# Second norm as token rows, queries masked by DMA, reciprocal products on GpSimd: a transformer block on one core of a Trainium2 chip

## The chip, the core and the metric

The kernel runs on one core of one Trainium2 chip. The metric is the device time of one execution in microseconds, as the median of the runs taken. Engines are named as in the profile: PE (TensorE, with PEld for its weight loads), DVE (VectorE), ACT (ScalarE), POOL (GpSimd) and SP (SyncE, which issues most of the DMAs). An engine takes its instructions strictly in the order in which they were issued, so an instruction that waits holds up all behind it.

## What is computed

With `x` of 2048 tokens by 512 features (bf16), the reference is a sum of three terms:

```python
xn = _layernorm(x)                              # no weights
return x + _A_ref(xn, A_wqkv, A_wo) + _B_ref(xn, B_w1, B_b1, B_w2, B_b2)

# A: softmax attention, 32 heads of 16 features, over all 2048 keys, then @ wo
# B: y = _layernorm(xn); h = gelu(y @ w1 + b1) with 1792 features; h @ w2 + b2
```

`B` norms `xn` a second time. Row by row this is a factor: with `v` the variance of a row of `x` and `r1 = (v + eps)^-1/2`, the row of `xn` is `(x - mean) * r1`, and `y = xn * r2` with `r2 = (v * r1^2 + eps)^-1/2`.

## The kernel before

**Tiling.** Tokens stand in 16 tiles of 128 (`x_sb`), the normed and transposed tokens in `xnT` (features on the partitions). Attention works in 32 groups `g`: 4 query chunks of 512 times 8 sets of 4 heads. A set pair `b` (8 heads) shares a projected key tile `kt`; its queries are projected once per query chunk into `qc`, and two copies in `qz` have the heads of the other set zeroed by `mask` (`build_q`, L921). A *unit* is the scores of one head of a group against 128 keys: one score matmul (L1063) into a PSUM bank of 128x512. Groups have 64 units each, 2048 in all.

**Two ways to the exponential.** ACT takes units in tiles of two or three banks: one ACTIVATE of 1024 or 1536 columns writes `p_sb` (`build_tile`, L1223 to L1295). DVE takes four units (one key tile of 4 heads) at a time: four times L1365 turns scores into int16 that read as float16 are a coarse exponential, and three times L1386 makes shifted copies of 2048 columns; PE then sums four terms in place of one (L1081). So a key tile costs PE one group of 4 concurrent value matmuls when ACT makes it, and four groups when DVE does. Which key tiles go to DVE is not fixed: `next_d` hands one out when DVE has a free buffer, ACT takes what is left.

**The other work** lies between: layer norm of the tokens in four steps of four tiles (`layernorm`, L737), key, value and query projections, two MLP stages of two token chunks each (`build_mlp`, L1521: the row factors `r2` are broadcast by 16 POOL products `rt` and a PE pass into `r2b`, then DVE makes `yT = xnT*r2b + xnT`; 14 matmul chains with `w_r`, a DVE add of the bias, gelu on ACT), the down projection, and the output. A group's end (`build_opost`, L1408): DVE copies the sums to `osb`, four DMAs by way of DRAM fetch the row of softmax sums, `rc` is its reciprocal, `rlb` the reciprocal spread over the partitions, and DVE multiplies `osb` by `rlb` (L1435) into `ont` or `ons`.

**What sets the order.** `_Plan` collects every operation with an engine, a duration, a priority and its dependences. `run` (L134) places them one at a time at the earliest start, by priority within a tolerance, and each engine's instructions are then issued in that order. `nudge` adds a seeded number to the priorities, one seed (`MIX`) for each group. Where PE would be idle for long, `fill` (L1688) puts in groups of 4 matmuls on zeros (L1718) that change no sum. The places that the change touches: `layernorm`, `f_r2` (L801), `late_dma` (L810), the first queries (`fq0`, `fq1`, L884 to L900), `build_q`, `build_opost`, `build_opost_last` (L1463), `build_mlp`, `build_final` (L1632).

## Time and profile before

| | |
|---|---|
| median of 3 runs | 769.67 us (769.47 to 770.04) |
| span of the profiled execution, first to last instruction | 767.6 us |
| busy, share of the span: PE, DVE, ACT, POOL | 96%, 92%, 97%, 8% |
| granted TensorE clock, mean | 0.998 |
| first and last exponential start on ACT | 12.01 us, 756.86 us |

The profiled execution has no time of its own beside its span; the runs are taken without the profiler. The span is 2.07 us below their median. What lies around the span (the start of the program, the landing of the last output) is taken as this 2.07 us. Busy time is the union of the instructions of an engine; matmuls overlap, so that a busy PE still has room.

### The profile page before, as it was taken

Reading aid. Unit: us, or ns where it says so; the run is one execution under the profiler, and the core shown is the slowest. Engines: PE = TensorE matmul, PEld = TensorE weight load, DVE = VectorE, ACT = ScalarE, POOL = GpSimd, SP = SyncE. Lnnn points to the kernel's source line nnn. Section 1 sums busy time; section 2 is a strip of 40 time slices with the busy share of each in tenths; the row PEclk is TensorE's granted clock in tenths of the full one; section 3 lists DMA queues with packets and bytes.
Section 4 is the critical chain, followed back from the end, with each engine's and each line's share of the span. In section 5 each row is a group of like instructions: output and inputs, shape, how many; then the busy total and the mean of one; then the engine's idle time right before and its main releaser. Section 6 shows DMA issues by size and latency. Waiting matters only on the chain.

```text
span 767.6 us, 23757 instructions
## 1 busy us (share of the span) xinstructions
PE 737.2 (96%) x10248; PEld 251.1 (33%) x10249; DVE 703.5 (92%) x1210; ACT 747.0 (97%) x655; POOL 62.0 (8%) x96
## 2 busy tenths in 40 slices
PE   8999999999999899999999999999999999999997
PEld 3443433343333232333233333222333333332332
DVE  7889999989999979989999968999999977888996
ACT  5999999999999999999999999999999999999995
POOL 2400100000042000001002010000001001100011
PEclk9999999999999999999999999999999999999999
DMA  6301011202142001122012132200211013200001
GB/s 192 106 3 32 20 51 41 52 18 51 47 115 71 16 5 51 37 56 64 21 43 61 31 75 62 60 9 16 62 41 37 19 29 79 68 12 25 5 18 44
DMA packets 59724, 35.43 MB, mean 46 GB/s; under 512 B 42404, under 2 KB 51428, under 8 KB 59616
## 3 DMA queue, kind: packets, MB, share of 16 engines
q1 hardware_dynamic: 52464, 23.91, 11.4%
q0 software_dynamic: 4608, 8.39, 4.8%
q8 instruction: 81, 1.33, 0.7%
q10 hardware_dynamic: 2544, 1.57, 0.7%
q14 instruction: 27, 0.22, 0.1%
HBM read 26.08 MB, written 2.61 MB: 37 GB/s over the span
## 4 chain that ended last, share of the span: by engine, by line
PE 38%; DVE 26%; ACT 25%; issue 10%; DMA 0%; POOL 0%; ACTq 0%; SPq 0%; DVEq 0%
ACT p_sb L1268 24%; PE ps L598 13%; PE ps L1081 12%; PE ps L1063 12%; DVE x_sb L1365 9%; DVE it L1386 8%; DVE it L1365 2%; DVE ht L1560 1%; ACT ht L1574 1%; DVE va L963 1%; DVE osb L1421 1%; DVE kt L915 1%; DMA x_sb<-in_A_x_dram 0%; PE ps L1718 0%; DVE stats L742 0%
## 5 line engine op out<-in xcount | busy, mean ns | idle before, releaser
L1268 ACT ACTIVATE p_sb<-ps 128x1536 bf16<-128x1536 f32 (+1 forms) x632 | 711.3, 1269 | 4.5 <-PE ps L1063 2.3
L1063 PE MATMUL ps<-qz,kt 32*128 32x512 bf16 x2048 | 314.6, 382 | 18.9 <-ACT p_sb L1268 9.1
L1365 DVE TENSOR_SCALAR x_sb<-ps 128x512 int16<-128x512 f32 x396 | 261.7, 680 | 18.4 <-PE ps L1063 18.1
L1386 DVE TENSOR_SCALAR it<-x_sb 128x2048 int16<-128x2048 int16 x297 | 197.9, 682 | 2.6 <-PE ps L1081 1.5
L1063 PEld LDWEIGHTS <-kt 32*128 32x128 bf16 x2048 | 86.5, 91 | 265.8 <-issue 258.9
L1081 PE MATMUL ps<-p_sb,va 128*32 128x512 bf16 x1552 | 151.6, 389 | 1.0 <-DVE x_sb L1365 0.2
L1081 PE MATMUL ps<-it,va 128*32 128x512 f16 x1588 | 128.5, 381 | 0.0
L1081 PEld LDWEIGHTS <-va 128*32 128x32 bf16 x3536 | 76.0, 94 | 129.7 <-issue 106.2
L1223 PE MATMUL ps<-ones_bf,zeros_bf 32*128 32x512 bf16 x291 | 106.1, 383 | 0.0
L1365 DVE TENSOR_SCALAR it<-ps 128x512 int16<-128x512 f32 x100 | 66.7, 680 | 2.4 <-PE ps L1063 2.3
L598 PE MATMUL ps<-w_sb,ht 128*32 128x512 bf16 x896 | 59.6, 381 | 0.2 <-DVE x_sb L1365 0.2
L598 PE MATMUL ps<-yT,w_r 128*32 128x512 bf16 x896 | 58.5, 381 | 0.6 <-DVE it L1365 0.3
L1386 DVE TENSOR_SCALAR it<-it 128x2048 int16<-128x2048 int16 x75 | 50.8, 683 | 1.5 <-PE ps L1081 1.0
L1560 DVE TENSOR_SCALAR ht<-ps,b_sb 128x512 bf16<-128x512 f32 x56 | 41.6, 743 | 5.6 <-PE ps L598 5.3
L1718 PE MATMUL ps<-ones_bf,zeros_bf 128*32 128x512 bf16 x488 | 41.9, 383 | 0.0
L1081 PE MATMUL ps<-x_sb,va 128*32 128x512 f16 x396 | 38.9, 383 | 0.1
L1223 PEld LDWEIGHTS <-zeros_bf 32*128 32x128 bf16 x291 | 26.1, 91 | 18.1 <-issue 17.3
L1456 POOL TENSOR_SCALAR okt<-lc 128x128 f32<-128x128 f32 (+1 forms) x4 | 4.0, 998 | 342.3 <-DMA lc<-ldram 342.3
L1584 POOL DMA_DIRECT2D wkv<-in_A_x_dram x16 | 12.4, 772 | 235.1 <-DVE ot L1598 224.6
L598 PEld LDWEIGHTS <-w_r 128*32 128x32 bf16 x896 | 21.6, 96 | 23.9 <-issue 9.6
L598 PEld LDWEIGHTS <-ht 128*32 128x32 bf16 x896 | 21.0, 96 | 22.5 <-issue 8.8
L1574 ACT ACTIVATE ht<-ht 128x3584 bf16<-128x3584 bf16 x8 | 24.9, 3178 | 0.0
(100 smaller groups left out, 352.5 us busy)
## 6 DMA issues: line engine op xcount, KB each, us to landing
rlb<-rdram SPq DMA_DIRECT2D x31, 256.0 KB
...
wkv<-in_A_x_dram POOLq DMA_DIRECT2D x16, 256.0 KB, 3.4
wkv<-in_B_b_dram POOLq DMA_DIRECT2D x16, 256.0 KB, 4.0
...
ont<-ons SPq DMA_DIRECT2D x60, 16.0 KB
```

What stands on the lines that cost most here:

```text
L598: I(nc.tensor.matmul(dst[32 * j:32 * j + 32], lhsT=lhsT[:, 32 * j:32 * j + 32], rhs=rhs, start=start, stop=stop, tile_position=(0, 32 * j)))
L915: I(nc.vector.tensor_copy(out=kt[:, b, c0:c0 + QW], in_=ps[:, pool.bank(key), :]))
L1063: I(nc.tensor.matmul(ps[:, bank, :], lhsT=kt[lo:lo + 32, s // 2, k * P:(k + 1) * P], rhs=qz[lo:lo + 32, (qt * NB + s // 2) % NQB, s % 2, : ...
L1081: I(nc.tensor.matmul(ps[32 * j:32 * j + 32, o_bank[g], :], lhsT=vals[:, h * VS:h * VS + 32], rhs=wts(j), start=pv_done[g] == 1, stop=end, ...
L1223: I(nc.tensor.matmul(ps[:, o_bank[g], :], lhsT=zeros_bf[32 * j:32 * j + 32, :], rhs=ones_bf[32 * j:32 * j + 32, :], start=False, stop=Fals ...
L1268: I(nc.scalar.activation(p_sb[:, s0:s1, :].rearrange("p a b -> p (a b)"), ps[:, b0:b0 + n, :].rearrange("p a b -> p (a b)"), AF.Exp, scale ...
L1365: I(nc.vector.tensor_scalar(out=ib[sl][:, j, :], in0=ps[:, pool.bank(key), :], scalar1=LEVEL, scalar2=0.0, op0=ALU.add, op1=ALU.max))
L1386: I(nc.vector.tensor_scalar(out=tb[x].rearrange("p j q -> p (j q)"), in0=ib[sl].rearrange("p j q -> p (j q)"), scalar1=float(SHIFT[t]), sc ...
L1560: I(nc.vector.tensor_scalar(out=hq[:, fc, :], in0=ps[:, misc.bank(key), :], scalar1=b1_sb[:, fc:fc + 1], scalar2=None, op0=ALU.add))
L1574: I(nc.scalar.activation(out=hv, in_=hv, func=AF.Gelu_apprx_tanh, scale=1.0))
L1584: xb_ = add("POOL", 1.0, lambda: I(nc.gpsimd.dma_start(out=acc[:, c, :], in_=x2[qi * P:(qi + 1) * P, :])), wait, pr - 30, lat=XL, nb=pr - 45)
L1718: I(nc.tensor.matmul(ps[32 * j:32 * j + 32, bank, :], lhsT=zeros_bf[:, 0:32], rhs=ones_bf[:], start=new, stop=new, tile_position=(0, 32 * ...
```

## The change

1. **Second norm token-major.** `r12 = r2*r1` is made on POOL for each four token tiles; DVE makes `ys = (x - mean)*r12` from `x_sb` (16 tiles of 128x512); POOL's queue writes them to DRAM (`ydram`), and one transposing DMA a chunk on SP's queue brings `yT` back. `rt`, `r2b`, its PE pass and the two DVE operations of 2048 columns a chunk are gone.
2. **Tokens of the fourth step** (tiles 12 to 15) go to `xnT` by four transposing DMAs, no longer by PE and a DVE copy. The transposes of tiles 4 to 11 use 4 matmuls of 128 columns each in place of 16 of 32.
3. **Masked queries by DMA.** `qc` is written to DRAM beside zeros (`zdram`), and two DMAs read it back with the rows of the other heads zero, into `qz`; the 30 DVE products are gone, 45 DMAs come onto SP's queue.
4. **Products with the reciprocals** (`osb*rlb`) go from DVE to POOL for the first 28 groups.
5. **First step.** ACT takes mean and variance of token tile 3; the first queries are split 384 and 128 columns over two banks, where ACT takes 128 columns of one copy; ACT issues three DMAs fewer.
6. **Last step.** Three of the four last output tiles get the sums by a PE pass and are copied by ACT (before: two); the check of the softmax sums is counted by PE, with less on POOL and no `okrow` on DVE.
7. **Order.** `MIX` is all zero; `PICK` names about a hundred operations each on DVE and PE that are to be taken at a given place in the order. Late loads wait for an exponential (`held`).

```diff
+                want = self.pick.get(e, {}).get(self.count[e])
+                if want is not None:
+                    t, op = next((c for c in every if c[1].seq == want), (t, op))
...
+    PICK = {
+        "DVE": {
+            3: 21, 16: 44, 19: 45, 22: 63, 27: 80, 29: 54, 34: 81, 36: 79, 38: 75, 39: 72, 40: 69,
...
+    def held(inst):
+
+        if len(exp_inst) > 1:
+            tc.add_manual_dep(inst.ins, exp_inst[-2].ins.name, SYNC_DEP, reason="its turn")
...
+            if t == 3:
+                def fs0():
+                    I(nc.scalar.activation(out=p_sb[:, 0, :], in_=x_sb[:, 3, :], func=AF.Copy,
+                                           scale=-D ** -1.5, accum_out=nm3[:]))
+
+                def fs1():
+                    I(nc.scalar.activation(out=p_sb[:, 1, :], in_=x_sb[:, 3, :], func=AF.Square,
+                                           bias=nm3[:], scale=D ** -0.5, accum_out=mv[:, 3, 1:2]))
...
+            if g in DG:
+                def ftd(t=t):
+                    I(nc.sync.dma_start_transpose(
+                        out=xnT[:, t // TQ, :, (t % TQ) * P:(t % TQ + 1) * P], in_=xn_r[:, t % 4, :]))
+                xn_op[t] = xt_op[t] = add("SP", 1.55, ftd, (xo,), pr, lat=TLAT)
+                continue
...
+            I(nc.gpsimd.tensor_tensor(out=r12[:, sl], in0=wv2[:, sl], in1=r1[:, sl], op=ALU.mult))
...
+            def fy(t=t):
+                I(nc.vector.tensor_scalar(
+                    out=ys[:, t % 2, :], in0=x_sb[:, t, :], scalar1=mv[:, t, 0:1],
+                    scalar2=r12[:, t:t + 1], op0=ALU.subtract, op1=ALU.mult))
+            y_op[t] = add("DVE", 0.33, fy, (r, yw_op.get(t - 2)), pr + t % 4 * 0.2)
+            yw_op[t] = add("POOL", 0.65, lambda t=t: I(nc.gpsimd.dma_start(
+                ydram[t * P:(t + 1) * P, :], ys[:, t % 2, :])), (y_op[t],), pr, lat=3.0)
...
-    qz_h = add("ACT", 0.31, fq1(QW // 2, QW), (q0, mk_mask), -30)
-    qz_op[0, 0, 0] = add("DVE", 0.36, fq0(0, 0, QW // 2), (q0, mk_mask, qz_h), -21)
+    qa = add("DVE", 0.47, fq0(0, key0, 0, QC), (qs[2], mk_mask), -21)
+    qz_op[0, 0, 0] = add("ACT", 0.3, fq1, (q0, mk_mask), -30)
...
+        w = dma("SP", zd.rearrange("(b z r) q -> b z r q", z=2, r=DH)[:, 0],
+                qc[:, n % 2, :], [e, mk_z[n % 2]] + qz_rd.get(n - 2, []), prio=pr - 600, lat=2.4)
...
-            def fd(par=par):
-                I(nc.vector.tensor_scalar(out=qz[:, n % NQB, par, :], in0=qc[:, n % 2, :],
-                                          scalar1=mask[:, par:par + 1], scalar2=None,
-                                          op0=ALU.mult))
-            o = add("DVE", dve(QW, 0.26), fd, [e, mk_mask] + old, pr + par - 600)
+            src = bass.AP(zd.tensor, zd.offset + par * DH * QW, [[4 * DH * QW, HS], [QW, 2 * DH], [1, QW]])
+            o = dma("SP", qz[:, n % NQB, par, :], src, [w] + old, prio=pr - 599 + par, lat=4.6)
...
-        e4 = add("DVE", dve(QW), lambda: I(nc.vector.tensor_tensor(
-            out=dst, in0=osb[:, i2, :], in1=rlb[:], op=ALU.mult)), [e3] + list(free),
-            pr - (1000 if g >= NG - LASTN else 0))
+        late = g >= NG - LASTN
+        e4 = add("DVE" if late else "POOL", dve(QW) if late else GMUL,
+                 lambda: I((nc.vector if late else nc.gpsimd).tensor_tensor(
+                     out=dst, in0=osb[:, i2, :], in1=rlb[:], op=ALU.mult)), [e3] + list(free),
+                 pr - (1000 if late else 0))
...
-        e3 = add("DVE", 0.2, lambda: I(nc.vector.tensor_reduce(
-            out=okrow[:], in_=okall[:], op=ALU.min, axis=AX.XY)), [e1, e2], pr - 10.0)
...
-        y = add("DVE", dve(4 * QW, 0.52), lambda: I(nc.vector.tensor_tensor(
-            out=yT[:], in0=xnT[:, qt, :, :],
-            in1=r2b[:].unsqueeze(1).to_broadcast([P, JC, QW]), op=ALU.mult)),
...
+        y = add("SP", 3.4, lambda: I(nc.sync.dma_start_transpose(
+            out=yT[:], in_=ydram[qt * QW:(qt + 1) * QW, :])),
+            y_use + [yw_op[4 * qt + i] for i in range(4)] + list(xn_op.values()), lo - 8, lat=YLAT,
+            nb=lo - 12)
...
-            if c % 2 == 0:
-                dep = [add("PE", 0.9, fi, dep, pr - 20, acq=acq, mode="d")]
+            if c != 2:
+                dep = [add("PE", 0.6, fi, dep, pr - 20, acq=acq, mode="d")]
```

**How the instructions move.** Counted over the whole order of each engine, from the kernel before to the changed one: exponentials on ACT 632 to 623 (344 of 1024 columns and 288 of 1536 before; 339, 283 and one of 512 now), which are 1552 and 1528 units; L1365 on DVE 496 to 520 and L1386 372 to 390, which is 124 and 130 key tiles; value matmuls on PE 3536 to 3608; matmuls on zeros in `fill` 488 to 468. On SP's queue 281 rows become 335. On PE's order of the changed kernel, between the last matmul that reads the first chunk's `yT` and the first that reads the second chunk's there are 28 score matmuls; between the third and the fourth key chunk's first projection, 23; between a query pair's projection and the first score matmul that reads its `qz`, at least 46 (62 or more before).

*ACT at the start* (names: `nm` holds tile 3's negative mean, `mv` its variance, `qz` the masked queries), from the table load to the exponentials, before:

```order
L791 ACT_TABLE_LOAD
L791 CAST xnT<-ps 128x4x128 x3
L878 CAST kt<-ps 128x128
L893 ACTIVATE qz<-ps,maskq 128x256
L880 CAST kt<-ps 128x384
L1268 ACTIVATE p_sb<-ps 128x1024 x10
```

and in the changed kernel:

```order
L803 ACT_TABLE_LOAD
L803 ACTIVATE p_sb,nm_84<-x_sb 128x512
L807 ACTIVATE p_sb,mv<-x_sb,nm_84 128x512
L877 CAST xnT<-ps 128x4x128 x3
L979 CAST kt<-ps 128x128
L993 ACTIVATE qz<-ps,maskq 128x128
L981 CAST kt<-ps 128x384
L1374 ACTIVATE p_sb<-ps 128x1024 x14
```

Two statistics of tile 3 stand ahead of the copies, and ACT's share of the first queries is 128 columns in place of 256.

*DVE at the input of the second MLP chunk*, before (`x_sb` and `it` are the buffers of DVE's exponentials):

```order
L1386 TENSOR_SCALAR it<-x_sb 128x2048 x2
L1365 TENSOR_SCALAR x_sb<-ps 128x512
L1537 CAST r2b<-ps 128x512
L1539 TENSOR_TENSOR yT<-xnT,r2b 128x2048
L1365 TENSOR_SCALAR x_sb<-ps 128x512 x2
L1544 TENSOR_TENSOR yT<-yT,xnT 128x2048
```

and *SP* at the same place of the changed kernel, where the chunk's input is made:

```order
L1637 DMA_TRANSPOSE yT<-ydram 128x4x512
L737 DMA w_r<-in_B_w_dram 128x4x128
L737 DMA zdram<-qc 8x16x512
L737 DMA qz<-zdram 128x1x512 x2
L1529 DMA ldram<-osb 4x512
```

DVE has none of L1537, L1539 and L1544 any more; SP has a transposing DMA, and behind it the write and the two reads of a query pair.

*POOL after the first query chunk's check*, before:

```order
L1458 TENSOR_TENSOR okt<-okt 128x128
L1459 TENSOR_TENSOR okall<-okall,okt 128x128
L1584 DMA wkv<-in_A_x_dram 128x512
L1587 DMA wkv<-in_B_b_dram 128x512
```

and in the changed kernel:

```order
L1566 TENSOR_TENSOR okt<-okt 128x128
L1567 TENSOR_TENSOR okall<-okall,okt 128x128
L1543 TENSOR_TENSOR ons<-osb,rlb 128x512
L1543 TENSOR_TENSOR ont<-osb,rlb 128x512
L1679 DMA wkv<-in_A_x_dram 128x512
L1682 DMA wkv<-in_B_b_dram 128x512
```

28 such products of 128x512 stand in POOL's order now, one for each of the first 28 groups.

## Rows read from the trace of the kernel before

**Rows 1.** The page: span and busy time of each engine.

```profile
span 767.6 us, 23757 instructions
...
PE 737.2 (96%) x10248; PEld 251.1 (33%) x10249; DVE 703.5 (92%) x1210; ACT 747.0 (97%) x655; POOL 62.0 (8%) x96
```

**Rows 2.** Window of the exponentials: us, busy of PE, PEld, DVE, ACT, POOL; clock, DMA.

```profile
12.01:757.98 745.97, 724.12 (x10147) 245.19 (x10147) 690.54 (x1173) 741.75 (x646) 55.81 (x76) 1.00 0.17 43
```

**Rows 3.** The page's groups: xcount | busy us, mean ns | idle before, releaser.

```profile
L1268 ACT ACTIVATE p_sb<-ps 128x1536 bf16<-128x1536 f32 (+1 forms) x632 | 711.3, 1269 | 4.5 <-PE ps L1063 2.3
```

**Rows 4.** Timeline of ACT at the start: start us, us, what [idle before].

```profile
4.56 1.28 ACT L791 ACT_TABLE_LOAD   x1 [4.56 <-DMA x_sb<-in_A_x_dram]
...
9.42 0.58 ACT L791 CAST xnT<-ps 128x512 bf16<-128x512 f32 x1 [0.25 <-PE ps L603]
9.91 0.27 ACT L878 CAST kt<-ps 128x128 bf16<-128x128 f32 x1
10.54 0.47 ACT L893 ACTIVATE qz<-ps,maskq 128x256 bf16<-128x256 f32 x1 [0.36 <-PE ps L603]
```

**Rows 5.** The chain of waits at the start: start us, us, what.

```profile
6.28 0.61 DVE stats L742
...
6.91 0.19 DVE mv L743
```

**Rows 6.** Groups by line and shape, DVE's first queries.

```profile
L886 DVE TENSOR_SCALAR qz<-ps,mask 128x256 bf16<-128x256 f32 x1 | 0.5, 484 | 1.3 <-ACT qz L893 1.3
```

**Rows 7.** The chain of waits at the end.

```profile
761.67 0.58 DVE yT L1665
762.25 0.17 DVE okrow L1500
...
762.47 0.69 DVE yT L1665
```

**Rows 8.** Groups by line and shape on DVE, removed or added to.

```profile
L1365 DVE TENSOR_SCALAR x_sb<-ps 128x512 int16<-128x512 f32 x396 | 261.7, 680 | 18.4 <-PE ps L1063 18.1
L1386 DVE TENSOR_SCALAR it<-x_sb 128x2048 int16<-128x2048 int16 x297 | 197.9, 682 | 2.6 <-PE ps L1081 1.5
...
L1435 DVE TENSOR_TENSOR ont<-osb,rlb 128x512 bf16<-128x512 f32 x16 | 10.9, 680 | 0.0
...
L938 DVE TENSOR_SCALAR qz<-qc,mask 128x512 bf16<-128x512 bf16 x30 | 9.1, 346 | 0.2
...
L772 DVE TENSOR_SCALAR yT<-x_sb,mv,r 128x512 bf16<-128x512 bf16 x16 | 5.6, 405 | 0.6 <-POOL r L758 0.6
...
L1539 DVE TENSOR_TENSOR yT<-xnT,r2b 128x2048 bf16<-128x2048 bf16 x4 | 4.9, 1222 | 0.1
L1544 DVE TENSOR_TENSOR yT<-yT,xnT 128x2048 bf16<-128x2048 bf16 x4 | 4.9, 1214 | 0.0
```

**Rows 9.** Groups by line and shape, matmuls on zeros that fill PE.

```profile
L1718 PE MATMUL ps<-ones_bf,zeros_bf 128*32 128x512 bf16 x488 | 41.9, 383 | 0.0
```

**Rows 10.** One line each: duration ns min/median/max, first and last start us.

```profile
L1459 POOL TENSOR_TENSOR okall<-okall,okt x4: 455/603/782, 213.8 to 746.6; 128x128 f32<-128x128 f32 x3, 128x112 f32<-128x112 f32 x1
```

**Rows 11.** Groups by line and shape, POOL's smallest product.

```profile
L1495 POOL TENSOR_TENSOR okl<-okl 128x8 f32<-128x8 f32 x2 | 0.4, 202 | 0.2
```

**Rows 12.** DVE's shifted copies, as rows 10.

```profile
L1386 DVE TENSOR_SCALAR it<-x_sb x297: 620/681/942, 47.1 to 755.6; 128x2048 int16<-128x2048 int16 x149
```

**Rows 13.** Timeline where the two meet: start us, us, what.

```profile
213.66 1.51 DVE L1386 TENSOR_SCALAR it<-x_sb 128x2048 int16<-128x2048 int16 x2
...
213.83 0.78 POOL L1459 TENSOR_TENSOR okall<-okall,okt 128x128 f32<-128x128 f32 x1
```

**Rows 14.** A window in which POOL is busy throughout, as rows 2.

```profile
234.00:238.00 4.00, 3.86 (x60) 1.38 (x58) 3.73 (x7) 3.87 (x4) 4.00 (x5) 1.00 0.49 104
```

**Rows 15.** DMA issues on POOL's queue: count, KB each, median us to landing.

```profile
wkv<-in_B_b_dram POOLq DMA_DIRECT2D x16, 256.0 KB, 4.0
```

**Rows 16.** Score matmuls: duration ns min/median/max, first and last start us.

```profile
L1063 PE MATMUL ps<-qz,kt x2048: 371/384/386, 11.6 to 755.9; 32*128 32x512 bf16 x187
```

More of the change, by code (lines that the diff above doesn't have):

```diff
@@ L134, in run @@
     def run(self):
-        free = {e: 0.0 for e in self.ENGS}
+        free = self.free = {e: 0.0 for e in self.ENGS}
+        self.count = {e: 0 for e in self.ENGS}
         ready = self.ready = {e: [] for e in self.ENGS}
@@ L215 @@
     pe_log = ()
+    pick = {}
     nq = 0
@@ L565 @@
     xn_r = yT
-    rt = const.tile([P, 4, P], BF, name="rt")
-    r2b = const.tile([P, QW], BF, name="r2b")
+    ys = const.tile([P, 2, D], BF, name="ys")
+    r12 = const.tile([P, NT], F32, name="r12")
     ht = const.tile([P, 2, FC, QW], BF, name="ht")
@@ L740, in layernorm, with fs2 @@
         for t in tt:
+            if t == 3:
[5 more added lines that the diff above has]
+                                           bias=nm3[:], scale=D ** -0.5, accum_out=mv[:, 3, 1:2]))
+                def fs2():
+                    I(nc.gpsimd.tensor_scalar(out=mv[:, 3, 0:1], in0=nm3[:], scalar1=-D ** 0.5,
+                                              scalar2=None, op0=ALU.mult))
+                s0 = add("ACT", 0.75, fs0, [ld_x[3]], -60, nb=4.1)
+                st_op[3] = add("ACT", 0.75, fs1, [s0], -60)
+                mean3.append(add("POOL", 0.25, fs2, [s0], -35))
+                continue
             def fst(t=t):
@@ L759, in frs @@
                                           op=ALU.pow))
-            r = add("POOL" if g else "DVE", 0.4 if g else 0.12, fes, [st_op[t] for t in range(sl.start, sl.stop)],
+            r = add("POOL" if g else "DVE", 0.4 if g else 0.12, fes, [st_op[t] for t in range(sl.start, sl.stop)]
+,
                     pr - (0 if g else 20))
+            if a == 0:
+                r.outs.append(st_op[2])
+                st_op[2].ndeps += 1
             r = add("POOL", 1.0 if g else 0.75, frs, [r, mk_half], pr)
@@ L920 @@
     qc_use = {}
+    qz_rd = {}
+    mk_z0 = add("POOL", 0.9, lambda: I(nc.gpsimd.memset(ons[:], 0.0)), (), 0.0)
+    mk_z = [add("POOL", 0.65, lambda n=n: I(nc.gpsimd.dma_start(
+        zdram[n].rearrange("(e p) q -> p e q", e=2), ons[:])), (mk_z0,), 10.0, lat=3.0, nb=16.0)
+        for n in range(2)]
     def build_q(qt, b):
@@ L1668, in fe @@
                     I(nc.scalar.copy(out=yT[:, c, :], in_=ps[:, pool.bank(key), :]))
-            outs.append(add("DVE" if c % 2 else "ACT", dve(D), fe, [m] + y_use, pr,
+            outs.append(add("DVE" if c == 2 else "ACT", dve(D), fe, [m] + y_use, pr,
                             rel=(pool.giver(key),)))
```

161 lines of the change are left out of this document (83 added, 78 removed), and 35 rows, old and new, of the table PICK.

## Prediction

> **What bounds the kernel now.** I read the page first, then the windows, the groups by line, the two ends of the chain of waits, and last the few places where POOL works. The page gives PE 96%, ACT 97% and DVE 92% of a span of 767.6 us [rows 1]; three engines are close to full, so the shares do not say which one sets the time. The window of the exponentials does: from 12.01 to 757.98 us ACT is busy for 741.75 of 745.97 us, 99.4% [rows 2], while PE is idle for 22 us and DVE for 55 us. And ACT's exponentials sat idle for only 4.5 us in the whole run, start included [rows 3]. So between its first and its last exponential this kernel is a queue of work on ACT, and time goes where ACT's work goes, as long as PE and DVE hand it scores in time. Outside the window lie 12.0 us ahead (a chain of waits through DVE, POOL, PE and ACT) and 9.6 us behind.
>
> PE's 97% inside the window is not all work: 488 matmuls on zeros, 122 groups of 4, run only where PE would be idle [rows 9]. DVE has room, but not much: its waits for PE before L1365 alone are 18.4 us [rows 8].
>
> **The change, part by part.** All against the span of 767.6 us; the runs' median lies 2.07 us above it, and I add that at the end.
>
> *Work moved off ACT: -11.0 us.* ACT's 632 exponentials take 711.3 us [rows 3] for the 1552 units of the order, 0.458 us a unit. The changed order has 1528. 24 x 0.458 = 11.0. This is fixed when the program is built; what can fail is only that ACT waits more.
>
> *What pays for it on DVE.* Gone: 28 products of `osb` by `rlb` at 0.680 (19.0), 30 masked copies (9.1), the two large operations of `yT` (4.9 + 4.9) [rows 8]; 4 copies to `r2b` and 4 of `xnT`, which read PSUM like L1365, at its 0.68 (5.4). Together 43.3. Added: 16 `ys` tiles of the size and kind of L772 (5.6 in all), 24 of L1365 at 261.7/396 = 0.661 (15.9), 18 of L1386 at 197.9/297 = 0.666 (12.0) [rows 8]; together 33.5. DVE's work falls by 9.8 to 693.7 us, and on a span near 756 its share stays at 92%. So DVE can do the six more key tiles, with no more and no less room than now.
>
> *PE.* 72 more value matmuls, 18 groups; nine score passes fewer, 16 matmul groups for `r2b` and the transposes of tiles 12 to 15 gone. I set this at nothing: the cover is the filling, 122 groups before and 117 after [rows 9]; if it were gone, 18 groups at the 41.9/122 = 0.34 us that a filling group is recorded with would cost 6 us at most.
>
> *The first step: -1.5 us.* Tile 3's statistics leave the chain (0.61 + 0.19 = 0.8) [rows 5]. ACT now takes them, with two operations of 512 columns; the copy of that size there takes 0.58 [rows 4]. They are hidden if they start before DVE is through with tile 2. The table load, which now starts at 4.56 [rows 4] behind six DMA issues of ACT, has three fewer ahead of it, so I count the whole 0.8; if it stayed where it is, 4.56 + 1.28 + 2 x 0.58 = 7.0 would be DVE's own end (7.1) and nothing would be won. Behind the last tile stand ACT's 256 columns (0.47) [rows 4] and, waiting for them, DVE's 256 (0.48) [rows 6]. In their place stand ACT's 128 columns, near the 0.27 of the 128-column copy [rows 4], while DVE's 384 are done earlier. That is 0.7. Bounds: 0.5 to 2.0 in all.
>
> *The last step: -0.3 us.* The chain ends with two outputs on DVE and the check between them (0.58 + 0.17 + 0.69) [rows 7]. Now one is on DVE beside one on ACT, and the check is off. I take half of what could go (0.17 + 0.58), because ACT has two copies in a row; the third PE pass lies in PE's wait for DVE. Bounds: 0 to 0.75.
>
> *Products on POOL: +1.2 us.* The trace has no product of 512 columns on POOL. One of 128 columns takes 0.455 at the least [rows 10], one of 8 takes 0.20 [rows 11]: 2.1 ns a column, 1.27 us for 512, 28 times (36 us; POOL has 700 us free). Nobody waits for one directly: before, the same product on DVE was put off by its low priority. What they cost is their effect on DVE. Where a POOL product met DVE's shifted copy, both got longer: the product 0.78 in place of 0.455, and the longest copy is 0.94 against a median of 0.68 [rows 10, 12, 13]. From below, the window in which POOL was busy for all of 4.00 us lost 0.13 us of ACT [rows 14]; 36/4 x 0.13 = 1.2. From above, a copy starts every 755/390 = 1.9 us, so 1.27/1.9 = 0.66 of the products meet one, for 0.63 us on average: 0.42 each, 11.7 us of DVE, all of it passed on. I take 1.2, because it is the one row in which ACT's loss stands beside the meeting.
>
> *DMAs in place of copies: 0.* A query pair now goes to DRAM and back. The nearest rows are POOL's DMAs of 256 KB, 4.0 us from issue to landing [rows 15]; a write and a read are 8 us, with three issues 10. The cover is at least 46 score matmuls at (755.9 - 11.6)/2048 = 0.363 us [rows 16], 16.7 us. The transposing DMAs have no row here. Doubling 4.0 for 512 KB gives 8 against a cover of 28 x 0.363 = 10.2 at the second MLP chunk; the other chunks have more. The fourth key chunk has 23 x 0.363 = 8.3 for four DMAs of 128 KB, half the size of that row, two of which are issued before the last tiles are ready. From above they cost what the third rival says. SP's waits grow with 54 more rows, but what stands behind them are loads of the next `w_r` and rows of sums that have a group's time.
>
> Sum: 767.6 - 11.0 - 1.5 - 0.3 + 1.2 = 756.0 of span, and 2.07 around it: **758.1 us**.
>
> **Rivals.**
>
> *1. Half of it is eaten.* Twice over, the spare time of DVE is used: by the meetings with POOL, and in the first 50 us, where `ys` has two buffers and each waits for the DMA two tiles back (4.0 us on POOL's queue [rows 15]). If half of the 11.7 us of DVE's delays reach ACT (+5.9 in place of 1.2) and the `ys` waits cost 2, the time is 758.1 + 4.7 + 2 = 765. For it speaks that DVE has no more room than now; against it, that ACT lost nothing like that while DVE waited 18.4 us for PE [rows 8]. Chance 0.17.
>
> *2. Slower: POOL's products hold DVE, DVE holds PE.* PE takes its instructions in order. If each product delays a shifted copy, PE waits at the value matmuls that read it, and the scores for ACT stand behind them. It decides from (11.0 + 1.5 + 0.3)/28 = 0.46 us a product. If each met a copy, at 0.63: 28 x 0.63 = 17.6, and the time is 767.6 - 12.8 + 17.6 + 2.1 = 774.5. For it: the stretched product and copy [rows 10, 12]; against it: in the window in which POOL was never idle ACT lost 0.13 of 4 us [rows 14]. Chance 0.08. [...]
>
> *3. Slower: PE waits for a transposing DMA.* It takes the place of the PE pass and the DVE operations. If such a DMA took five times as long as the plain one of 4.0 us [rows 15], 20 us for a chunk of 512 KB, PE would wait 20 - 10.2 = 9.8 us at the second MLP chunk and about 20 - 8.3 = 11.7 at the fourth key chunk: 758.1 + 21.5 = 779.6. It decides when the two together are 11.5 us late. Chance 0.05. [...]
>
> *That the change doesn't do what it says* is possible at the start alone (the table load): 0.8 us, inside the forecast.
>
> **How the numbers follow.** Forecast 0.70: 753.5 to 762. It goes down to 753.5 if ACT also loses less than the 4.2 us that it is now idle in the window [rows 2], and up to 762 with the bounds of the start and a third of DVE's delays. Rival 1 has 0.17 (763 to 769), rival 2 0.08, rival 3 0.05. Two runs can be told apart from about 0.2%, 1.5 us: faster is below 768.1, slower above 771.2. Faster: 0.70 and 0.14 of rival 1, 0.84. Same: 0.05, the rest of rival 1 and the mild end of the others. Slower: 0.11. The range reaches over most of rival 1, to 767, and leaves out about 0.17.
>
> **What would show it.** Right: 622 or 623 exponentials with about 700 us on ACT; the first at about 10.5 us in place of 12.0; ACT still over 99% busy between its first and last; POOL's products near 1.3 to 1.6 us; PE's idle time before matmuls that read `qz`, `xnT` or `yT` without a DMA as the releaser. Wrong: a longer idle time of ACT before L1374 (rivals 1 and 2, where the DVE copies beside POOL's products are above 0.9 us in the mean), or one wait of PE of many microseconds released by a DMA (rival 3).

## The result, and the profile after

The changed kernel takes 776.14 us (median of six runs, 773.73 to 778.53), the kernel before 769.61 (769.41 to 770.04). The ratio is 1.0083, 95% interval 1.0064 to 1.0101: slower, where 758.1 was forecast (range 753.5 to 767.0). Runs of one kernel spread: the changed kernel's six over 4.8 us, the kernel before's over 0.6, and two of e17's twelve below, at a mean granted clock of 0.982, lie 10 us above the others' middle.

The page of the changed kernel, and its row of the exponentials (below, against [rows 1, 3]):

```profile
span 774.2 us, 23564 instructions
...
PE 736.0 (95%) x10064; PEld 247.5 (32%) x10066; DVE 708.5 (92%) x1191; ACT 740.1 (96%) x651; POOL 105.5 (14%) x139
...
L1374 ACT ACTIVATE p_sb<-ps 128x1536 bf16<-128x1536 f32 (+1 forms) x623 | 702.2, 1257 | 18.7 <-PE ps L1169 16.0
```

The 623 exponentials came as forecast, but ACT now idles 18.7 us before them (4.5 before), 16.0 of it for score matmuls. DVE has 708.5 us of work where the forecast counted 693.7. The window of the exponentials (columns as [rows 2]):

```profile
11.47:763.06 751.59, 722.39 (x9958) 241.34 (x9958) 695.80 (x1156) 732.87 (x637) 95.40 (x114) 1.00 0.23 57
```

The span misses the forecast of 756.0 by 18.2 us, in three parts. **Ahead of the window:** the first exponential starts at 11.47, not 10.5: +0.95. **Behind it:** 774.2 - 763.06 = 11.14, not 767.6 - 757.98 - 0.3 = 9.32: +1.8. **In it:** 751.59 where 745.97 - 11.0 + 1.2 = 736.17 was forecast: +15.4. Of these, 13.3 are idle time of ACT (18.72, against the 4.22 of [rows 2] and the 1.2 added), the other 2.1 work of ACT (down by 8.9, not 11.0).

Where ACT idles, by stretches of the window: length less ACT's busy time, the fourth busy column. First the kernel before, then the changed one.

```profile
12.10:80.00 67.90, 65.49 (x1306) 26.95 (x1294) 61.58 (x119) 66.95 (x71) 10.79 (x17) 1.00 0.17 49
80.00:170.00 90.00, 87.43 (x1573) 33.49 (x1573) 84.70 (x142) 89.69 (x80) 2.58 (x4) 1.00 0.14 37
170.00:380.00 210.00, 203.16 (x2581) 65.44 (x2571) 197.78 (x335) 209.26 (x177) 19.46 (x24) 1.00 0.19 48
380.00:430.00 50.00, 48.69 (x637) 15.77 (x632) 47.25 (x77) 49.91 (x45) 4.45 (x8) 1.00 0.22 51
430.00:750.00 320.00, 311.30 (x3979) 100.91 (x3978) 292.25 (x493) 317.87 (x271) 18.52 (x24) 1.00 0.15 38
```

```profile
12.10:80.00 67.90, 64.24 (x1178) 25.85 (x1167) 63.52 (x127) 65.28 (x69) 18.95 (x37) 1.00 0.43 108
80.00:170.00 90.00, 85.59 (x1460) 32.21 (x1456) 82.98 (x134) 86.62 (x77) 7.54 (x6) 1.00 0.17 46
170.00:380.00 210.00, 202.05 (x2602) 65.41 (x2595) 197.41 (x322) 206.53 (x175) 21.20 (x21) 1.00 0.19 50
380.00:430.00 50.00, 45.35 (x550) 13.74 (x546) 46.23 (x74) 45.11 (x40) 11.52 (x14) 0.97 0.48 101
430.00:750.00 320.00, 311.65 (x4017) 99.59 (x4009) 298.43 (x491) 315.65 (x269) 36.19 (x36) 1.00 0.19 49
```

Idle: 1.0, 0.3, 0.7, 0.1, 2.1 before; 2.6, 3.4, 3.5, 4.9, 4.4 now. A slow loss from the first product (82 us) on, and one short loss of 4.9 us near 400 us, where the DMA share is 0.48 and the granted clock 0.97. Two theories came out of this.

**L: a product on POOL holds DVE's shifted copy.** Groups by shape, and the copies' line (min/median/max in ns; before [rows 8, 12]):

```profile
L1543 POOL TENSOR_TENSOR ont<-osb,rlb 128x512 bf16<-128x512 f32 x14 | 19.8, 1418 | 217.3 <-DMA rlb<-rdram 196.4 <-DMA wo_l<-in_A_wo_dram 20.9
L1492 DVE TENSOR_SCALAR it<-x_sb 128x2048 int16<-128x2048 int16 x309 | 218.0, 722 | 4.1 <-PE ps L1187 2.3
```

```profile
L1492 DVE TENSOR_SCALAR it<-x_sb x309: 626/686/1773, 44.8 to 756.0; 128x2048 int16<-128x2048 int16 x155
```

The timeline of the first product (start us, us; idle before) shows one meeting and where it leads:

```profile
82.23 1.27 POOL L1543 TENSOR_TENSOR ont<-osb,rlb 128x512 bf16<-128x512 f32 x1 [6.75 <-DMA rlb<-rdram]
82.28 1.77 DVE L1492 TENSOR_SCALAR it<-x_sb 128x2048 int16<-128x2048 int16 x1
...
83.97 1.28 DVE L1471 TENSOR_SCALAR x_sb<-ps 128x512 int16<-128x512 f32 x2
84.71 0.37 PE L1169 MATMUL ps<-qz,kt 32*128 32x512 bf16 x1 [0.94 <-DVE x_sb L1471]
```

The copy starts 0.05 us behind the product and ends 0.55 us after the product does. The conversions L1471 behind it are late, so the PSUM bank that they empty is late, and PE's next score matmul waits 0.94 us for it. Counted along the trace, 18 of the 28 products have such a copy beside them, of 0.88 to 1.77 us: 24.3 us, 12.0 more than 18 at the median. A copy that was under way before its product began took its usual 0.68 to 0.70 us.

**S: transfers crowd each other near 400 us.** The timeline there, POOL and its queue, SP's queue, DVE, then ACT:

```profile
388.23 1.26 POOL L1543 TENSOR_TENSOR ont<-osb,rlb 128x512 bf16<-128x512 f32 x1 [22.20 <-DMA rlb<-rdram]
389.44 1.80 POOL L1679 DMA_DIRECT2D wkv<-in_A_x_dram  x3
395.99 2.99 POOL L1682 DMA_DIRECT2D wkv<-in_B_b_dram  x3 [4.76 <-DMA wkv<-in_A_x_dram]
...
391.82 5.43 SPq L1637 DMA_TRANSPOSE yT<-ydram  x1
397.36 2.80 SPq L737 DMA_DIRECT2D w_r<-in_B_w_dram  x3
400.20 0.56 SPq L1529 DMA_DIRECT2D ldram<-osb  x1
404.36 0.35 SPq L1531 DMA_DIRECT2D lc<-ldram  x1
...
406.03 0.25 DVE L1534 RECIPROCAL rc<-lc 128x16 f32<-128x16 f32 x1 [1.61 <-DMA lc<-ldram]
...
403.09 4.62 ACT L1374 ACTIVATE p_sb<-ps 128x1536 bf16<-128x1536 f32 x4 [0.99 <-PE ps L1169]
410.14 1.45 ACT L1374 ACTIVATE p_sb<-ps 128x1536 bf16<-128x1536 f32 x1 [2.43 <-PE ps L1169]
```

Six loads of 256 KB for the output sums (`wkv`, reused as `acc`) go out in one burst of 10 us behind a product that stood at the head of POOL's queue for 22.2 us; beside them run the third transposing load of `yT` and four loads of `w_r`. The 8 KB store of the row sums (`ldram`) takes 4.1 us, the reciprocal waits, and DVE, which has it next in its order, idles 1.61 us ahead of it. ACT goes idle twice; the second gap (2.43 us) follows this wait, the first (0.99) lies ahead of it. On PE, and a window over the time after its second wait (columns as [rows 2]):

```profile
401.61 1.05 PE L606 MATMUL ps<-yT,w_r 128*32 128x512 bf16 x16 [0.99 <-DVE it L1492]
...
407.84 1.66 PE L606 MATMUL ps<-yT,w_r 128*32 128x512 bf16 x16 [1.61 <-DVE it L1471]
```

```profile
408.10:411.50 3.40, 3.40 (x34) 0.79 (x26) 3.06 (x6) 1.35 (x1) 1.12 (x3) 0.51 0.38 100
```

Two things stand in these rows beside the crowd. PE's first wait is put down to a copy, but the same matmul also waits for the third load of `yT`, which by the trace's semaphores landed in full at 401.48, 0.13 us ahead of it and 9.7 us after its issue (4.3 to 6.0 us for the other three loads): PE waited for that load. And after PE's second wait its granted clock, 1.00 from 5.4 us until then, was at half from 408.1 to 411.5 us (0.51 in the row above); 16 matmuls that had taken 1.05 us took 1.66. The kernel before has no such stretch ahead of 763 us. How much of the short loss this is was not tried: in e1, where the clock stays full here, ACT still idles 3.6 of the 4.9 us.

### The profile page after: what moved, and what is told of

Read it like the earlier page. It is cut to its first block, busy times and chain, and to the rows that moved or that the text cites. A ratio compares the mean times of both kernels' runs of the same rounds, so it can differ in the third digit from the quotient of the medians.

```text
span 774.2 us, 23564 instructions
## 1 busy us (share of the span) xinstructions
PE 736.0 (95%) x10064; PEld 247.5 (32%) x10066; DVE 708.5 (92%) x1191; ACT 740.1 (96%) x651; POOL 105.5 (14%) x139
## 4 chain that ended last, share of the span: by engine, by line
PE 45%; DVE 24%; ACT 20%; issue 8%; DMA 2%; SPq 0%; POOL 0%; DVEq 0%; ACTq 0%
ACT p_sb L1374 20%; PE ps L1169 15%; PE ps L1187 15%; PE ps L606 13%; DVE x_sb L1471 10%; DVE it L1492 8%; DVE it L1471 1%; DMA lc<-ldram 1%; DMA ldram<-osb 1%; DVE ht L1655 1%; PE ps L1813 1%; DVE osb L1527 1%; PE ps L1742 0%; PE ps L611 0%; DVE ot L1693 0%
## 5 line engine op out<-in xcount | busy, mean ns | idle before, releaser
L1374 ACT ACTIVATE p_sb<-ps 128x1536 bf16<-128x1536 f32 (+1 forms) x623 | 702.2, 1257 | 18.7 <-PE ps L1169 16.0
L1169 PE MATMUL ps<-qz,kt 32*128 32x512 bf16 x2048 | 307.0, 383 | 20.0 <-ACT p_sb L1374 7.1
L1471 DVE TENSOR_SCALAR x_sb<-ps 128x512 int16<-128x512 f32 x412 | 274.1, 684 | 14.3 <-PE ps L1169 12.7
L1492 DVE TENSOR_SCALAR it<-x_sb 128x2048 int16<-128x2048 int16 x309 | 218.0, 722 | 4.1 <-PE ps L1187 2.3
L1169 PEld LDWEIGHTS <-kt 32*128 32x128 bf16 x2048 | 80.6, 91 | 257.7 <-issue 250.9
L1187 PE MATMUL ps<-it,va 128*32 128x512 f16 x1668 | 135.8, 381 | 2.1 <-DVE it L1492 2.0
L1329 PE MATMUL ps<-ones_bf,zeros_bf 32*128 32x512 bf16 x272 | 100.0, 383 | 0.0
L1471 DVE TENSOR_SCALAR it<-ps 128x512 int16<-128x512 f32 x108 | 72.9, 684 | 8.2 <-PE ps L1169 8.0
L1543 POOL TENSOR_TENSOR ons<-osb,rlb 128x512 bf16<-128x512 f32 x14 | 19.4, 1383 | 238.1 <-DMA rlb<-rdram 145.6
L1543 POOL TENSOR_TENSOR ont<-osb,rlb 128x512 bf16<-128x512 f32 x14 | 19.8, 1418 | 217.3 <-DMA rlb<-rdram 196.4
```

Source lines behind the costliest of these rows:

```text
L1169: I(nc.tensor.matmul(ps[:, bank, :], lhsT=kt[lo:lo + 32, s // 2, k * P:(k + 1) * P], rhs=qz[lo:lo + 32, (qt * NB + s // 2) % NQB, s % 2, : ...
L1187: I(nc.tensor.matmul(ps[32 * j:32 * j + 32, o_bank[g], :], lhsT=vals[:, h * VS:h * VS + 32], rhs=wts(j), start=pv_done[g] == 1, stop=end, ...
L1329: I(nc.tensor.matmul(ps[:, o_bank[g], :], lhsT=zeros_bf[32 * j:32 * j + 32, :], rhs=ones_bf[32 * j:32 * j + 32, :], start=False, stop=Fals ...
L1374: exp_inst.append(I(nc.scalar.activation(p_sb[:, s0:s1, :].rearrange("p a b -> p (a b)"), ps[:, b0:b0 + n, :].rearrange("p a b -> p (a b)" ...
L1471: I(nc.vector.tensor_scalar(out=ib[sl][:, j, :], in0=ps[:, pool.bank(key), :], scalar1=LEVEL, scalar2=0.0, op0=ALU.add, op1=ALU.max))
L1492: I(nc.vector.tensor_scalar(out=tb[x].rearrange("p j q -> p (j q)"), in0=ib[sl].rearrange("p j q -> p (j q)"), scalar1=float(SHIFT[t]), sc ...
```

## Experiments

Except for e5 and e6, each run keeps the planned order and changes only what an operation issues, or where a load is issued. Medians, and ratios to the kernel before (95%) of five rounds each:

| run | us | ratio |
|---|---|---|
| e1 20 products cut to 32 columns | 771.36 | 1.0018 (1.0009 to 1.0027) |
| e2 plain loads for transposing | 775.20 | 1.0077 (1.0054 to 1.0101) |
| e3 products on DVE in place | 774.61 | 1.0066 (1.0054 to 1.0078) |
| e4 before, products on POOL | 773.69 | 1.0057 (1.0044 to 1.0069) |
| e5 no picks | 787.89 | 1.0239 (1.0211 to 1.0266) |
| e6 no picks, products on DVE | 782.14 | 1.0172 (1.0138 to 1.0207) |
| e7 products in 4 pieces | 770.70 | 1.0011 (0.9999 to 1.0024) |
| e8 no third load | 774.49 | 1.0063 (1.0040 to 1.0086) |
| e9 4 pieces, third load early | 768.95 | 0.9989 (0.9980 to 0.9998) |
| e10 8 pieces, third load early | 766.75 | 0.9955 (0.9942 to 0.9968) |
| e11 third load early | 773.90 | 1.0058 (1.0044 to 1.0072) |
| e12 loads of sums early | 773.22 | 1.0044 (1.0031 to 1.0058) |
| e13 8 pieces, loads of sums early | 764.45 | 0.9934 (0.9920 to 0.9947) |
| e14 e13 and third load early | 765.68 | 0.9944 (0.9931 to 0.9958) |
| e15 e14 without most mask transfers | 764.96 | 0.9938 (0.9924 to 0.9951) |
| e16 e13 and the fill moved | 764.42 | 0.9928 (0.9915 to 0.9941) |
| e17 before, 8 pieces on POOL | 771.16 | 1.0043 (1.0015 to 1.0071) |

### The products (e1, e3, e4, e7, e17)

```diff
+        cw = QW if late or (g < 2 * NON and not odd) else 32
...
-                     out=dst, in0=osb[:, i2, :], in1=rlb[:], op=ALU.mult)), [e3] + list(free),
+                     out=dst[:, 0:cw], in0=osb[:, i2, 0:cw], in1=rlb[:, 0:cw], op=ALU.mult)),
+                 [e3] + list(free),
```

> The changed kernel with its order kept, instruction for instruction; 20 of the 28 products on GpSimd are cut from 512 columns to 32 (the output is then not the reference's; the work left out is 20 x 480 columns of GpSimd). Theory L (a product holds up the 128x2048 copy that meets it on VectorE, and the delay runs on to ScalarE): the copies' mean falls from 722 to about 690 ns, ScalarE's idle time falls by 20/28 of the roughly 6.5 us that stand within 6 us of a product, so 776.1 becomes about 771.5. Theory S (the loss comes from the DMA queue on SyncE, its transposing loads and the waits behind them): 775 to 777, the copies faster but ScalarE's waits where they were. Theory O (the written-out order has no slack for any deviation from its model): between the two, and the early waits before 80 us remain.

771.36: theory L's number. The early waits before 80 us (ACT idles 2.6 us) and the ones near 400 us (3.6 us) remain, as S and O had it; they are not small beside the 4.8 us that the products gave back.

e3 issues the same product on DVE (`I.cur = "DVE"; I(nc.vector.tensor_tensor(...))`) where the plan has it on POOL.

> The changed kernel with its order kept; the 28 products stand on VectorE at the place in time at which GpSimd was to do them. VectorE gets 28 x 0.68 = 19.1 us of work and loses the stretch of its copies (309 x 0.04 + 81 x 0.02 = 14 us). Theory L: about the same, 775 to 778, with a 128x2048 copy back at 682 ns. Theory S: the time stays as well, since no transfer moves, or grows by some of the 5 us: 776 to 781. It tells how large a product on GpSimd is for VectorE: if it costs as much there as on VectorE itself, the two times agree within 2 us.

774.61, within 2 us of the changed kernel; the longest copy is 0.82 us. The loads of the output sums no longer stand behind products here: they go out from 321 to 360 us, and ACT idles 0.9 us from 380 to 430 us. So this is DVE's products against the holds and the burst together; e12 below, with whole products on POOL and no burst, is 1.4 us faster. A whole product on POOL cost here about what it cost on DVE (776.14 and 774.61 us): little or nothing was won by moving it.

e4 does the reverse to the kernel before (`I.cur = "POOL"; I(nc.gpsimd.tensor_tensor(...))` for the products of all but the last four groups: 28 in the trace, where the expectation counts 27).

> The kernel before with its order kept; 27 of its 31 products (all but the last four) go to GpSimd, nothing else. VectorE loses 27 x 0.68 = 18.4 us of work. Theory L: 27 meetings stretch the copies by some 0.5 us each (13 us of VectorE busy time back), and the stalls that reach ScalarE cost 2 to 5 us: 771 to 775 against 769.6. Theory S: no change or a little faster, 768 to 769.8.

773.69, slower by 4.2 us though 28 products, 19 us, are taken off DVE. Its copies:

```profile
L1386 DVE TENSOR_SCALAR it<-x_sb x297: 622/683/1762, 47.0 to 758.9; 128x2048 int16<-128x2048 int16 x149
```

Nothing but the products moved, and the longest copy goes from 942 [rows 12] to 1762 ns. That is L in a kernel without any other part of the change; near 400 us ACT loses nothing here (0.2 us from 380 to 430).

```diff
+        w = QW if late else QW // 4
+        for c in range(0, QW, w):
+            I((nc.vector if late else nc.gpsimd).tensor_tensor(
+                out=dst[:, c:c + w], in0=osb[:, i2, c:c + w], in1=rlb[:, c:c + w], op=ALU.mult))
```

> The changed kernel with its order kept; each of the 28 products on GpSimd is issued as four of 128 columns. Theory L, with a product holding the copy for its whole instruction: a copy waits for a quarter at most, so the stretch falls from 14 us to 3 to 5, the copies' mean to 690 to 695 ns, and 776.1 becomes 767 to 771. If GpSimd's work slows the copies by its amount and not by holding them for one instruction: the copies stay at 715 to 730 and the time at 774 to 778.

770.70, in the range (the copies' mean fell to 701 ns, less than expected). The lines of copies and products of this run:

```profile
L1492 DVE TENSOR_SCALAR it<-x_sb x309: 621/682/998, 45.0 to 751.4; 128x2048 int16<-128x2048 int16 x155
...
L1519 POOL TENSOR_TENSOR ont<-osb,rlb x56: 445/458/1004, 82.5 to 668.4; 128x128 bf16<-128x128 f32 x56
```

The same columns are multiplied, POOL is busy for longer (64.2 us in place of 39.2), and the loss shrinks: the longest copy is 1.00 us in place of 1.77, while now pieces wait for copies (1004 against 458). What counts in these runs is the length of one instruction, not POOL's work: the longest copy falls with the piece, and the eight products that took 1.42 to 1.82 us in the changed kernel each began together with a copy or up to 0.4 us into one. What in the hardware holds the later of the two, no run shows.

e17 is e4 with eight pieces.

> The kernel before with its order kept and 27 products on GpSimd, now in eight pieces of 64 columns; whole, they gave 773.7 against 769.6. Theory L: most of the 4.1 us go, 769.5 to 771. If products on GpSimd cost by their amount: 773 to 774.

771.16, 2.5 of the 4.1 us back, 0.2 outside the expected range; a rest of 1.6 us stays.

### The transfers (e2, e8, e11, e12)

```diff
-        y = add("SP", 3.4, lambda: I(nc.sync.dma_start_transpose(
-            out=yT[:], in_=ydram[qt * QW:(qt + 1) * QW, :])),
+        y = add("SP", 3.4, lambda: I(nc.sync.dma_start(
+            yT[:], ydram[qt * QW:(qt + 1) * QW, :].rearrange("(j p) d -> p j d", p=P))),
```

> The changed kernel with its order kept; the four transposing loads of the second MLP's input and the four transposes of the last group's normalized tokens are plain loads of the same bytes, so the transposition is left out. Theory S: SyncE is held 0.5 to 0.7 us a load in place of 1.2 to 5.4, the wait of the reciprocal near 405 us (1.6 us) and ScalarE's 2.4 us and 1.0 us gaps there are gone, 776.1 becomes 771 to 772. Theory L: 775 to 777, since no product is touched.

775.20, no difference from 776.14: S in this form falls. SP was free at 395.9 us, but the row sums' store still took 5.5 us. It is not the transposition that holds the store, but what else is being moved. The third load itself landed 7.5 us after its issue here (9.7 when transposing), and PE did not wait for it.

The four loads of `xnT` from `yT` (`ftd`) are changed likewise. In e8 the third load's function issues nothing.

> The changed kernel with its order kept; the third of the four loads of the second MLP's input (near 392 us, 512 KB) is left out, so that MLP step works on the step before's input. Theory S' (this load crowds the queue in which the row sums' small transfers wait): the transfer of the row sums near 400 us lands in 2 us again, the reciprocal does not wait, and ScalarE's gaps of 1.0, 2.4, 0.3 and 0.6 us between 403 and 422 us are gone: 776.1 becomes 771 to 773. If the other weight loads of that place do it: 775 to 777.

774.49, a miss of 1.5 us. The gaps between 403 and 422 us did shrink, from 4.4 us to 0.2 and 0.8, and between 380 and 430 us ACT idles 1.4 us in place of 4.9; but ahead of 380 us it had idled 10.4 us in place of 9.5, and it idles more afterwards (5.1 in place of 4.4 to 750 us). e11 keeps the load and issues it with the 13th product.

> The changed kernel with its order kept and its whole products on GpSimd; the third load of the second MLP's input is issued at the 13th product, near 341 us. Theory S' alone: the row sums' transfer near 400 us lands in 2 us, ScalarE's gaps between 403 and 422 us (4.4 us) go, 776.1 becomes 771 to 773. If the other loads make the crowd: 775 to 777.

773.90, 0.9 above the expected range; gaps of 1.5 and 0.8 us are left. In e12 the three pairs of loads (`soon = TQ <= qi < TQ + 3`) issue nothing at their places in the plan, and go out behind an output of the step before:

```diff
+    def out_sum(dst, key, c, qi):
+        I(nc.vector.tensor_tensor(out=dst, in0=ps[:, misc.bank(key), :], in1=acc[:, c, :], op=ALU.add))
+        if qi < 3:
+            I.cur = "POOL"
+            acc_load(qi + TQ, c, 0)
+            acc_load(qi + TQ, c, 1)
```

> The changed kernel with its order kept but for GpSimd's queue: three pairs of loads of the output sums (256 KB each), which stand behind a product that waits until 388 us for its reciprocals and then go out together, are issued right after the outputs that free their places (320, 339, 356 us). Theory G (products that wait on GpSimd hold back the loads behind them, and the burst at 389 to 399 us delays the row sums' transfers): ScalarE's gaps between 403 and 422 us, 4.4 us together, shrink to 1 or 2, and 776.1 becomes 772 to 774. If the crowd is made by the weight loads on SyncE's queue: 775 to 777.

773.22, in the range of G. The stretch near 400 us of this run:

```profile
380.00:430.00 50.00, 48.01 (x599) 15.04 (x595) 49.27 (x82) 49.11 (x44) 7.19 (x8) 1.00 0.31 75
```

ACT idles 0.9 us there in place of 4.9. Yet the time falls by 2.9 only. The traced execution is the longest of the five (775.3 us): from 80 to 170 us ACT idles 5.1 us in place of 3.4, with the clock at half from 94.1 to 97.5 (0.98 in the mean of these 90 us), and from 430 to 750 us 5.6 in place of 4.4. Whether products cost more there because DVE has less time in hand once ACT is not late is not shown.

### The order (e5, e6)

e5 has `PICK = {}`; e6 also plans the products on DVE.

> The changed kernel without its table of picked places: the planner's own rule sets the order, and gives ScalarE 1548 score units in place of 1528 (20 x 0.42 = 8.4 us of ScalarE work come back). Theory L (products on GpSimd hold up copies on VectorE): the copies' mean stays at 710 to 730 ns; with more score units on ScalarE, VectorE has some 23 us less to do and can swallow part of the stretch: 772 to 778. Theory O (the picked order itself is what loses, by leaving no slack): ScalarE's idle time falls from 18.7 to under 10 us, so 776.1 + 8.4 - 9 = 775 or less; without the picks nothing else changes. If the picks are worth what they take off ScalarE and the loss comes from elsewhere: 780 to 784.

> The changed kernel without picks and with all 31 products planned and run on VectorE; 1552 score units on ScalarE as in the kernel before. What is left of the change is the token-major second norm, the masked queries by DMA and the new first and last steps. Theory L: no copy is stretched (682 to 690 ns), ScalarE idles 5 to 9 us, so about the kernel before: 767 to 773, faster than the run without picks by 4 to 8. Theory S (transfers) : ScalarE's waits do not depend on the products, 773 to 778.

787.89 and 782.14, both outside, both too slow. Theory O falls: the picked order is worth 11.8 us on the chip. The step from e5 to e6, 5.8 us, goes the way of the products (longest copy 2.21 and 0.86 us), but e6's order is planned anew, so it is not theirs alone. Why e6 stays 12 us above the kernel before is not taken apart. Its exponentials wait 13.6 us, 5.1 of them from 380 to 430 us, where PE waits 3.84 us for the third load of `yT` and the clock is then at half from 399.2 to 402.6 us; and the tail is longer:

```profile
L1337 ACT ACTIVATE p_sb<-ps 128x1536 bf16<-128x1536 f32 (+1 forms) x632 | 712.0, 1268 | 13.6 <-PE ps L1132 11.1 <-ACT p_sb L1337 0.4
```

```profile
398.94 1.70 PE L606 MATMUL ps<-yT,w_r 128*32 128x512 bf16 x16 [3.84 <-DMA yT<-ydram]
```

### Together (e9, e10, e13 to e16)

> The changed kernel with its order kept, the products in four pieces of 128 columns, and the third load of the second MLP's input issued at the 13th product (near 341 us) in place of 392 us, where that step's input tile has been free since about 290 us. Both theories together: the split alone gave 770.7; ScalarE's gaps of 1.3, 2.7, 0.5, 0.5 and 0.4 us between 399 and 419 us, 5 us together, go with the load: 765.5 to 767.5, below the kernel before (769.5). If the crowd at 392 us is made by the other loads there: 769.5 to 771.

> As the run with four pieces and the early load, with eight pieces of 64 columns. If a copy waits for one piece of a product, the hold halves once more: the copies' mean falls from 701 towards 690 ns, and the time by 1 to 2 us, to 764 to 766.5. If each piece holds some copy anew, or GpSimd's products become so long (8 x 0.3 to 0.5 us) that what waits for them is late: the same or 1 to 3 us slower than with four pieces.

768.95 and 766.75, 1.5 and 0.3 us above their ranges: a gap of 2.0 us at 404 to 406 us stayed, since the burst of loads (192 and 217 GB/s from 390 to 400 us) was not touched. Eight pieces gain 2.2 us more than four.

> As the run with the loads of the output sums moved, and the products in eight pieces of 64 columns. Theories L and G together: 770.7 was the split in four alone, some 769 to 770 in eight; without the gaps around 405 us 765 to 767. If only L holds: 769 to 771.

764.45, 0.5 below the range and faster than both kernels: 0.9934 of the kernel before, and 11.7 us below the changed one. Its page, and the stretches as above:

```profile
span 761.6 us, 23764 instructions
...
PE 732.5 (96%) x10066; PEld 248.1 (33%) x10066; DVE 699.2 (92%) x1191; ACT 737.3 (97%) x651; POOL 152.3 (20%) x335
```

```profile
11.45:750.33 738.88, 718.10 (x9959) 241.36 (x9958) 686.45 (x1156) 730.08 (x637) 142.15 (x310) 1.00 0.23 58
...
12.10:80.00 67.90, 64.40 (x1179) 25.83 (x1167) 63.53 (x127) 65.29 (x69) 18.97 (x37) 1.00 0.42 108
80.00:170.00 90.00, 87.13 (x1476) 32.59 (x1476) 83.25 (x138) 88.39 (x78) 14.77 (x41) 1.00 0.17 46
170.00:380.00 210.00, 204.78 (x2650) 66.40 (x2638) 197.51 (x327) 208.87 (x178) 41.32 (x90) 1.00 0.22 58
380.00:430.00 50.00, 48.17 (x613) 15.54 (x605) 49.19 (x82) 49.70 (x45) 13.92 (x28) 1.00 0.34 82
430.00:750.00 320.00, 312.63 (x4044) 100.50 (x4040) 292.47 (x484) 316.84 (x272) 53.16 (x115) 1.00 0.18 47
```

ACT's idle time is 2.6, 1.6, 1.1, 0.3 and 3.2 us: all that the changed kernel lost between 80 and 430 us is gone but some 2 us. Its work is 730.08, 11.7 below [rows 2]. Taken apart, four pieces gave 5.4 us, eight 2.2 more and the burst 2.9: 10.5 of the 11.7 us by which the time fell.

> Products in eight pieces, the third load of the second MLP's input at the 13th product, and the three loads of the output sums moved. The load moved alone left a gap of 2.2 us near 405 us, when 192 GB/s were moved from 390 to 400 us. Theory G: that gap goes as well, 763 to 765.5. If the weight loads alone fill the queue: 766 to 768, as with the early load and eight pieces.

> As the run with all three edits, and from the fifth group of queries on their three transfers are left out (the scores then use an earlier group's queries; 11 of 15 stores and 22 of 30 loads of 128 KB are missing, nothing else). Theory Q (the masked queries' loads stand in SyncE's queue ahead of the row sums' transfers, as near 141 us, where one took 4.6 us): the remaining waits of VectorE on those transfers and ScalarE's gaps behind them go, 2 to 4 us less than with the masks: 760 to 763. If they cost nothing, as the prediction had it: the same within 1 us.

765.68 (0.2 above its range) and 764.96. The early third load adds nothing once the sums' loads are spread: its trace idles 0.3 us from 380 to 430 us, as e13's does, and 3.8 in place of 1.6 us from 80 to 170, where the clock was at half from 148.1 to 151.5. Theory Q falls: without most of the mask transfers the time moves by 0.7 us, inside the runs' spread, and the prediction's nothing for them stands.

e16 moves the fill of `wo_l` behind the start, so that the fill of `ons` comes earlier.

> As the run with eight pieces and the loads of the output sums moved, and one more edit at the start: the fill of the last output weights (0.94 us on GpSimd at 2.10 us) is moved to the first product, in eight pieces, so that the new fill of 1024 columns no longer runs at 2.99 us, where VectorE's scaling of the masks took 0.92 us in place of 0.17. If that meeting is what the start lost, the scaling takes 0.17 again and the first exponential starts 0.4 to 0.8 us earlier than 11.45: 10.7 to 11.1, and the time is 763.7 to 764.4. If the chain at the start waits for something else (the transfers of the tokens): 11.4 as before.

Half of it came true. The scaling of the masks beside POOL's fill in the changed kernel, and without it in e16:

```profile
2.98 0.94 POOL L1021 MEMSET ons<- 128x1024 bf16 x1
3.03 0.92 DVE L778 TENSOR_SCALAR maskq<-mask 128x2 f32<-128x2 f32 x1
```

```profile
3.04 0.17 DVE L778 TENSOR_SCALAR maskq<-mask 128x2 f32<-128x2 f32 x1
3.41 0.69 DVE L819 BATCH_NORM_STATS2 stats<-x_sb 128x6 f32<-128x512 bf16 x1 [0.20 <-DMA x_sb<-in_A_x_dram]
...
11.57 1.94 ACT L1374 ACTIVATE p_sb<-ps 128x1024 bf16<-128x1024 f32 x2
```

The hold is gone, but DVE then waits for the tokens, the first exponential starts no earlier, and the time is the same (764.42). The meeting at the start costs nothing.

## Why the prediction was wrong

- **The step that failed is "Products on POOL: +1.2 us".** Both ends were worked out, 1.2 and 11.7, and the lower was taken. The upper one was nearly exact as to DVE: 0.66 of the products were to meet a copy and 18 of 28 did, for 12.0 us of stretch where 11.7 was put. How much of it is passed on to the time: four pieces give back 5.4 us (e7), eight 8.8 with the burst of loads out of the way (e12 to e13). The lower end came from a window in which POOL was busy throughout [rows 14], scaled by POOL's busy time. e7 shows why that can't be scaled: a meeting costs by the length of the one instruction that is in the way (longest copy 1.77 us beside products of 512 columns, 1.00 beside pieces of 128). And meetings are what counts: in that window, beside a load and four operations of 0.9 us each, DVE ran one shifted copy (0.83 us) in 4 us, where the forecast itself has one every 1.9 us. The upper end would still have given 768.6.
- **"Nobody waits for one directly" failed too.** The loads of the output sums stand behind the products on POOL's queue. A product that waited 22.2 us for its reciprocals held six loads back until they went out together: 2.9 us alone (e12).
- **What is left.** Of the 18.0 us between 758.1 and 776.14, e13 takes back 11.7, holds and burst. Of its other 6.3, its trace has 0.9 ahead of the window, 2.7 in it (738.88 against 736.17) and 1.9 behind it; the rest lies between its traced execution and its median, and around the span (1.8 us in the changed kernel's run, not 2.07).
- **"Work moved off ACT: -11.0 us" was right.** 623 exponentials; ACT's work is 11.7 us lower in e13. In the changed kernel it is 8.9 only: one exponential overlaps the next by less when there is a wait between them, and counted along the trace the overlaps are 80.8 us, against 89.5 in e13.
- **DVE's balance was nearly right without the holds:** 693.7 was put, 699.2 are there in e13, 708.5 with whole products.
- **DMAs in place of copies: 0** holds for the masked queries (e15), and as far as times can tell for the transposition (e2). But PE does wait for a transposing load, at the third chunk, which was put among those with "more" cover: 1.0 us in the changed kernel, 1.5 in e7, 3.8 in e6. That what stands behind these transfers on SP "has a group's time" does not hold near 400 us; the crowd there is made by the burst and the third load together: taking either away shrinks ACT's idle time from 380 to 430 us, to 1.4 us (e8) and 0.9 (e12).
- **First step, -1.5: -0.55.** The chain of waits of the changed kernel at the start:

```profile
6.38 0.80 POOL r L835
...
7.20 0.99 DVE yT L852 x2
...
9.78 1.15 DVE qz L987 x2
```

  What follows the statistics starts 1.0 us earlier (6.38 in place of 7.38; 0.8 was put). But two tiles are normed on the chain where one was (0.42), and both of DVE's query products of 384 columns stand on it (1.15), where the forecast had them done beside PE.
- **Last step, -0.3: nothing.** From the end of the last exponential to the end of the flag it is 5.29 us, 5.23 before. What is longer comes after: 5.85 us from the flag to the end of the span in place of 4.43, in which no compute instruction runs. All runs of the changed kernel have it (11.1 to 11.6 us behind the last exponential), e4 and e17 do not (10.0 and 9.7). Why was not tried and stays open, as does the 1.7 us that ACT loses more ahead of 80 us, before any product; it is in all runs built on the changed kernel (2.7 us without the picks).
- **The rivals.** Rival 2 had the mechanism, the side, and 774.5, and was given 0.08. Its number is near 776.1 by luck in part: it put 17.6 us for the holds alone; the holds, the burst, the start and the end share what was lost. Rival 1's half (5.9 us) is less than the holds took, and of its `ys` waits none shows on DVE ahead of 81 us. Rival 3 came only in small: the loads of `yT` kept SP for 1.9 to 5.4 us and landed 4.3 to 9.7 us after their issue, not 20, and PE waited 1.0 us for one of them. The 20 us were the author's assumption, five times a plain load of 4.0 us; no run shows them. With plain loads in their place (e2), which landed 3.8 to 7.5 us after their issue, the time is 775.20 against 776.14.
